# First block of network 1 in one written list, and its last pair's down matrix by seven products of halves

## The chip, the core and the metric

The kernel runs on one core of one Trainium2 chip. The metric is the device time of one execution in microseconds. A core has TensorE (PE, matmuls; PEld is its weight load), VectorE (DVE), ScalarE (ACT), GpSimd (POOL) and SyncE (SP), each with its own instruction queue, and 16 DMA engines fed by queues, here those of SP and of ACT.

## The reference, cut to what matters

```python
# attention, B=8, H=8, S=576, D=64, in 9 chunks of 64 tokens
scores = q_c @ k_c.T / sqrt(D); attn = exp(scores - max); attn = attn / (sum + 1e-9); out = attn @ v_c
x = out.transpose(0, 2, 1, 3).reshape(4608, 512)
# network 1: d_model 512, d_ff 1536
xn = x / sqrt(mean(x * x) + 1e-6) * rms_g
x = (silu(xn @ w_gate) * (xn @ w_val)) @ w_out
# network 2: d_ff 2048
h = x @ w_in
return (h * clip(h + 3, 0, 6) / 6) @ w_out2
```

q, k, v and rms_g are float32, the weight matrices float64.

## The kernel before, in words

The 4608 tokens are nine blocks of 512. A block's x lies with its 512 channels on the partitions, in four pieces of 128 (KD = 4), and its 512 tokens on the free axis. Every matmul of the networks is done three times, to keep float32's digits: each operand is a high part rounded to fp32r and a low part, what the rounding left; the products are high by high, low by high and high by low. A column of 128 hidden units costs `mm_up` 3 x 4 matmuls of 128x512, and a row piece of w_out costs `mm_down_a` 3 x 4 too.

**Weights.** A weight piece is 512 KB of float64 words. `Prep` turns it into parts in four steps, each for a list of pieces: `mag` (ACT, L139, a Prelu on the high words), `bits` (DVE, L184, L186, L188, which clamp, shift and join the two words to float32), `hi` (ACT, L195, the high part) and `lo` (DVE, L204, the low part). Network 1 has 36 pieces: 12 of w_gate, 12 of w_val, 12 of w_out.

**Start.** Attention of the first four tiles of 128 tokens (`Att`, units 0 to 3) and the first weight pieces follow the list `START`, one method name with its unit's number per token, as `trans_qk0`; a token with w or W is a step of `Prep`, w for a pair of pieces, W for one. The loads follow the list `LOADS`. `heat` and `pad` are matmuls whose results nobody reads. The last steps of a tile are `mean` (sum of squares on TensorE), `root` (ACT), `inv` (DVE), `spread` (TensorE), `norm` (DVE), `hi` and `lo`, which write the parts XH and XL of x.

**Network 1.** The first three blocks run plainly, in a loop over 12 columns f: gate (G), Silu (S), value (V), product of both (M, DVE), its parts (`split_act`: A on ACT, L on DVE or GpSimd), and the down product (D) of the column before. After each third of a column `tick` issues what the `agenda` has for this tick: attention of later tiles, normalisation of later blocks, stores. In block 0 each tick also calls `prep_hook`, which steps the remaining weight pieces two at a time. The other six blocks are three pairs p = 0, 1, 2: two blocks of tokens at once, with the up matrices by seven products of halves in place of eight (`product`, L1029), for which sums and differences of operand halves are kept in DRAM beforehand (`ops`, d1) and loaded again as tiles "wo" (`Loads`, 512 KB each, on SP's queue). A pair is 66 ticks (PAIR), 42 of them up products. Its down matrix is plain: the 12 pieces of w_out are loaded again for each of the two blocks, 24 x 12 matmuls. The output of network 1 goes to DRAM (yd).

**Network 2.** Its first block is plain (`mm_up`, `mm_down_b`); the others run in pairs with seven products for the up and the down matrix (`product_down`, L1581). The operands for that (the `Stash`) are prepared during network 1's pairs, on ACT, DVE and POOL, and are stored from ACT's queue (L290, L294) and loaded again from SP's.

PSUM has eight banks of 128x512. Bank numbers of the plain path: ATT 0, GB 2, VB 3, YB 4.

## Time and profile before

| | us |
|---|---|
| median of 3 runs | 1655.03 (1654.75 to 1655.18) |
| profiled execution | 1654.2 |
| its span in the profile | 1652.4 |
| TensorE busy | 1640.0 (99%), 9920 matmuls |
| VectorE busy | 1030.2 (62%) |
| ScalarE busy | 846.1 (51%) |
| GpSimd busy | 453.4 (27%) |
| DMA | 375.08 MB, mean 227 GB/s |

The span runs from the first to the last recorded instruction; the profiled execution has 1.8 us around it. Busy shares are averages over stages: the start (0 to 44 us), block 0 (44 to 149), blocks 1 and 2 (to about 350), the three pairs (to 949), and network 2. PEclk is the share of full speed that TensorE's clock was granted. A row of the timeline says how long an operation took, and in brackets how long its engine had been idle before it and who released it.

### The profile page before, as it was taken

To read this page: it belongs to the slowest core of one execution; us is meant where nothing else is said; L and a number is where in the kernel's file an instruction comes from. 1 tells how busy PE (TensorE), PEld (TensorE's weight loads), DVE (VectorE), ACT (ScalarE), POOL (GpSimd) and SP (SyncE) were. 2 spreads that over 40 slices of the span, in tenths; PEclk is the share of its full clock that TensorE was granted. 3 is DMA by queue.
4 is the path that set the end of the run, shared out by engine and by line. 5 is a ranking of instruction groups with operands and counts; after the bars stand their busy time and mean duration, and the time that the engine had idled before them with its cause. 6 is when DMAs were issued, how large, how long until landed. Compare 5 with 4: busy or idle time off the path is not lost.

```text
span 1652.4 us, 26451 instructions
## 1 busy us (share of the span) xinstructions
PE 1640.0 (99%) x9920; PEld 1350.1 (82%) x9920; DVE 1030.2 (62%) x1533; ACT 846.1 (51%) x1409; POOL 453.4 (27%) x333
## 2 busy tenths in 40 slices
PE   8999999999999999999999999999999999999999
PEld 7788887888888888888888888888888888888887
DVE  6887566655575755748334388358746764875475
ACT  6885445355464454635444334455545544654553
POOL 1002434322226432354226522141024003301310
PEclk8999999999999999999999999999999999999999
DMA  9914776738976688865979676767876796788666
GB/s 303 277 44 100 212 208 204 224 135 248 314 263 226 208 286 289 274 210 199 346 241 327 260 268 205 228 192 249 219 216 219 214 243 197 224 222 231 196 194 163
DMA packets 336098, 375.08 MB, mean 227 GB/s; under 512 B 184289, under 2 KB 260065, under 8 KB 335841
## 3 DMA queue, kind: packets, MB, share of 16 engines
q1 hardware_dynamic: 266080, 302.32, 59.7%
q10 hardware_dynamic: 69888, 71.06, 12.6%
q8 instruction: 79, 1.29, 0.3%
q14 instruction: 51, 0.41, 0.1%
HBM read 292.55 MB, written 80.74 MB: 226 GB/s over the span
## 4 chain that ended last, share of the span: by engine, by line
PE 95%; DVE 2%; DMA 1%; ACT 1%; issue 0%; SPq 0%; POOL 0%; DVEq 0%; POOLq 0%
PE PS L1029 39%; PE PS L1581 18%; PE PS L1018 13%; PE PS L1043 6%; PE PS L1044 6%; PE PS L1046 6%; PE PS L923 1%; PE PS L850 1%; DMA wo<-ops 1%; PE PS L832 1%; PE PS L1051 1%; PE PS L1055 1%; PE PS L1052 1%; PE PS L1783 1%; PE PS L794 0%
## 5 line engine op out<-in xcount | busy, mean ns | idle before, releaser
L1029 PE MATMUL PS<-xu,wo 128*128 128x512 f32 x1512 | 350.2, 391 | 0.5 <-DVE xu L1243 0.5
L1029 PEld LDWEIGHTS PS<-xu,wo 128*128 128x128 f32 x1512 | 282.1, 188 | 59.8 <-DVE xu L1243 0.9
L1029 PE MATMUL PS<-xo,wq 128*128 128x512 f32 x1344 | 305.3, 389 | 0.0
L1581 PE MATMUL PS<-gs,wq 128*128 128x512 f32 x1296 | 295.3, 389 | 0.0
L1029 PEld LDWEIGHTS PS<-xo,wq 128*128 128x128 f32 x1344 | 252.3, 188 | 52.4
L1581 PEld LDWEIGHTS PS<-gs,wq 128*128 128x128 f32 x1296 | 242.9, 188 | 51.7 <-DVE gs L1575 1.2
L1018 PE MATMUL PS<-XH,w 128*128 128x512 f32 x576 | 147.9, 399 | 2.7 <-ACT XH L656 1.9
L1018 PEld LDWEIGHTS PS<-XH,w 128*128 128x128 f32 x576 | 107.1, 190 | 26.4 <-ACT XH L656 2.2
L1043 PE MATMUL PS<-gs,wd 128*128 128x512 f32 x288 | 113.2, 393 | 0.0
L1044 PE MATMUL PS<-gs,wd 128*128 128x512 f32 x288 | 112.2, 389 | 0.0
L1074 POOL TENSOR_TENSOR al<-sg,ah 128x512 fp32r<-128x512 f32 x40 | 55.8, 1396 | 154.6 <-ACT ah L1072 150.3
L1353 POOL TENSOR_TENSOR gs<-gu,gs 128x512 fp32r<-128x512 f32 x60 | 84.3, 1423 | 45.9 <-ACT gs L1352 39.9
L1357 DVE TENSOR_TENSOR gu<-gu,PS 128x512 f32<-128x512 f32 x60 | 41.1, 686 | 83.0 <-ACT gu L1439 45.8
L1649 POOL TENSOR_TENSOR gt<-gx 128x512 f32<-128x512 f32 x8 | 10.3, 1290 | 296.5 <-DVE gx L1646 296.5
L1575 DVE TENSOR_TENSOR gs<-gu,gs 128x512 fp32r<-128x512 f32 x88 | 67.9, 791 | 32.0 <-ACT gs L1574 31.7
L1574 ACT CAST gs<-gt 128x512 fp32r<-128x512 f32 x96 | 58.1, 623 | 43.9 <-DVE gt L1718 33.5
L1512 DVE SCALAR_TENSOR_TENSOR gu<-gu,PS 128x512 f32<-128x512 f32 x48 | 32.8, 684 | 72.9 <-ACT gu L1509 72.9
L1018 PE MATMUL PS<-XL,w 128*128 128x512 f32 x288 | 77.9, 393 | 0.0
L1046 PE MATMUL PS<-gs,wd 128*128 128x512 f32 x288 | 77.0, 389 | 0.0
L1072 ACT CAST ah<-sg 128x512 fp32r<-128x512 f32 x52 | 32.4, 624 | 84.7 <-DVE sg L1330 53.2
L1574 ACT CAST gs<-gu 128x512 fp32r<-128x512 f32 x96 | 57.4, 621 | 25.2 <-DVE gs L1575 17.7
L1649 POOL TENSOR_TENSOR gt<-gu 128x512 f32<-128x512 f32 x24 | 32.5, 1355 | 129.0 <-DVE gu L1646 124.9
(249 smaller groups left out, 2823.8 us busy)
## 6 DMA issues: line engine op xcount, KB each, us to landing
wq<-stash_in SPq DMA_DIRECT2D x128, 512.0 KB
wo<-ops SPq DMA_DIRECT2D x126, 512.0 KB
wq<-sums_out SPq DMA_DIRECT2D x64, 512.0 KB
wq<-stash_out SPq DMA_DIRECT2D x48, 512.0 KB
wd<-keep_out SPq DMA_DIRECT2D x36, 512.0 KB
yd<-yst SPq DMA_DIRECT2D x18, 512.0 KB
ops<-w ACTq DMA_DIRECT2D x36, 256.0 KB
v<-in_v_dram SPq DMA_DIRECT2D x32, 256.0 KB
```

The costliest lines, as they stand in the source:

```text
L1018: nc.tensor.matmul(ps, w(wi, c), xs[c][xi], start=(i == 0), stop=(i == n - 1))
L1029: nc.tensor.matmul(PS[:, bank, :], op[:, wi, c * 128:(c + 1) * 128], x[xi][:, c, :], start=first and i == 0, stop=last and i == 5, skip_gr ...
L1043: nc.tensor.matmul(ps, wm[0], a[0], start=first, stop=False)
L1044: nc.tensor.matmul(ps, wm[1], a[0], start=False, stop=False)
L1046: nc.tensor.matmul(PS[:, banks[m], :], w[:, 0, m * 128:(m + 1) * 128], a[1], start=False, stop=last)
L1074: nc.gpsimd.tensor_tensor(lo, t, hi.bitcast(F32), op=ALU.subtract)
L1353: e.tensor_tensor(w[:, 1, :], t, w[:, 0, :].bitcast(F32), op=ALU.subtract)
L1357: nc.vector.tensor_tensor(o, x, y, op=op)
L1574: nc.scalar.copy(w[:, 0, :], x)
L1575: e.tensor_tensor(w[:, 1, :], x, w[:, 0, :].bitcast(F32), op=ALU.subtract)
L1581: nc.tensor.matmul(PS[:, banks[m], :], op[:, wi, m * 128:(m + 1) * 128], x[xi], start=first and (wi, xi) == (0, 0), stop=False, skip_group ...
L1649: nc.gpsimd.tensor_tensor(slot(i, "t"), slot(i, "12"), slot(i, "11"), op=ALU.subtract)
```

## The change

It has three parts.

1. *Start and block 0.* `LOADS` and `START` are written anew: q and k of all four tiles first, v and weight pieces after. `heat` and `pad` give way to `warm`, one 128x256 matmul on ones, 79 times. `mean` multiplies by 128 columns of ones, not one. The ones are written by DVE, not GpSimd, and the load of rms_g goes behind the first pieces. Block 0 leaves the loop: every gate, value, product, Prep step (one piece at a time) and tick stands in the list `FIRST`. The tables `SHARE_V` and `LOW_V` say which tiles' `share` and `lo` run on DVE.
2. *Pair 2's down matrix.* `OutSums` (six of them, two pieces of w_out each) loads w_out's parts, adds them, forms the sums of halves on DVE, splits them (ACT, DVE) and stores them from ACT's queue (e1). In pair 2 the down matrix is 42 steps of `product_down`, six matmuls each; the hidden values are combined by `sums_g` on GpSimd and by `feed` on DVE, split by `split_by` on ACT and DVE, and partial outputs are kept and added by `kept` and `more`.
3. *Network 2's first block* uses other PSUM banks, and the loads of the stash's out halves 4 to 7 move into it from pair 2.

```diff
-    w q0 q1 v0 q2 w q3 w v2 v1 v3 w w w w w w w w w w w w w
+    q1 q3 q0 q2 w v3 w g w w v1 v0 v2 w w w w w w w w w w w w
@@ START
...
+    share0 share2 warm2 warm2 warm2 warm2 warm2 warm2 warm2 warm2 warm2 warm2 warm2 warm2 warm2 warm2 warm2 warm2
+    warm2 warm2 warm2 warm2 mean3 trans_p0 warm2 warm2 warm2 warm2 warm2 warm2 warm2 warm2 values1 trans_p2 Wm2
...
+FIRST = """
+    G0 V0 T T S0 T M0 G1 T T Wm9 Wm8 Wm7 Wh4 T Wh5 A0 Wh6 Wb8 Wl4 Wb9 L0 Wl5 Wm10 Wm11 Wm13 S1 Wh9 V1 T M1 Wb10
...
+SHARE_V, LOW_V = (), (2, 3)
@@ class Prep
-            stage(ids)
-            self.seen |= {(stage, i) for i in ids}
+            {"m": self.mag, "b": self.bits, "h": self.hi, "l": self.lo}[op[1]]([int(op[2:])])
+    class OutSums:
...
+        def load(self):
+            self.r = [self.buf(tag) for tag in ("q", "k")]
+            for z in range(2):
+                nc.sync.dma_start(out=self.r[z], in_=o1[2 * self.i + z])
...
+        def split(self, z):
+            if z == 0:
+                self.w = [self.buf(tag, F32R) for tag in ("kT", "p")]
+            w, u = self.w[z], self.u[:, z, :]
+            nc.scalar.copy(w[:, 0, :], u)
+            nc.vector.tensor_tensor(w[:, 1, :], u, w[:, 0, :].bitcast(F32), op=ALU.subtract)
+
+        def keep(self):
+            for z in range(2):
+                for y in range(2):
+                    nc.scalar.dma_start(
+                        out=e1[:, 2 * z:2 * z + 2, self.i, y, :],
+                        in_=self.w[z].bitcast(F32)[:, y, :].rearrange("p (k n) -> p k n", k=2),
+                    )
+
+        def plan(self, t0):
+            for d, fn, *args in (
+                (0, self.load), (2, self.whole), (3, self.sums), (4, self.split, 0), (4, self.split, 1), (5, self.keep)
+            ):
+                at(t0 + d, fn, *args, turn=3)
@@ class Att
-            self.ms = PS[:, self.bank, 0:1]
+            self.ms = PS[:, self.bank, 0:128]
-        def heat(self):
-            for _ in range(2):
-                nc.tensor.matmul(PS[:, self.bank + 1, 256:512], ones_r, XL[:, 0, 0:256], start=True, stop=True)
+        def warm(self):
+            nc.tensor.matmul(PS[:, self.bank + 1, 256:512], ones_r[:, 0:128], ones_r, start=True, stop=True)
@@ the pairs
+        for i in range(NI):
+            OutSums(i).plan(P0 + 2 * PAIR - 3 + 4 * i)
+        def split_by(e, x):
+            w = wp.tile([128, 2, N], F32R, tag="w", name="gs")
+            nc.scalar.copy(w[:, 0, :], x)
+            e.tensor_tensor(w[:, 1, :], x, w[:, 0, :].bitcast(F32), op=ALU.subtract)
+            return w[:, 0, :], w[:, 1, :]
+            def sums_g(i):
+                nc.gpsimd.tensor_tensor(slot(i, "t"), slot(i, "12"), slot(i, "11"), op=ALU.subtract)
+                x = slot(i, "12")
+                nc.gpsimd.tensor_tensor(x, slot(i, "22"), x, op=ALU.subtract)
+            steps = [
+                (pr, i)
+                for pr, span in (
+                    (1, range(NI)), (5, range(NI)), (6, range(NI)), (2, range(4)), (7, range(NI)),
+                    (2, range(4, NI)), (3, range(NI)), (4, range(NI)),
+                )
+                for i in span
+            ]
+            for n, (pr, i) in enumerate(steps):
...
+                product_down(bk[z], loads.t[key][:, i % 2], nx.popleft(), pr in (1, 5) and i == 0)
+                if i % 2 == 1:
+                    loads.t.pop(key)
                     loads.ahead(1)
...
+                feed(n + 4)
@@ network 2, first block
-            bank = 6 + n % 2
+            bank = 2 + n % 2
-            if n == 4:
-                for z in range(2):
-                    stash[NQ - 1].fetch_out(z)
+            if n < 8:
+                stash[4 + n // 2].fetch_out(n % 2)
-                mm_down_b(W["out2", fs[n - 1]], prev, n == 1, False, base=2)
+                mm_down_b(W["out2", fs[n - 1]], prev, n == 1, False, base=4)
```

How TensorE's instructions stand at the handover from attention to network 1. L617 is `mean`, L593 `values`, L636 `spread`, and L1018 the first column G0. Before:

```order
L593 MATMUL PS<-pT,v 64x64 x16
L636 MATMUL PS<-pT,ones 128x128
L617 MATMUL PS<-ones,pT 128x1 x4
L636 MATMUL PS<-pT,ones 128x128
L617 MATMUL PS<-ones,pT 128x1 x4
L636 MATMUL PS<-pT,ones 128x128 x2
L1018 MATMUL PS<-XH,w 128x512 x8
```

With the change, where L669 is `mean`, L688 `spread`, L698 `warm` and L1063 the first column:

```order
L688 MATMUL PS<-pT,ones_r 128x128
L669 MATMUL PS<-ones_r,pT 128x128 x8
L698 MATMUL PS<-ones_r 128x256 x3
L688 MATMUL PS<-pT,ones_r 128x128
L669 MATMUL PS<-ones_r,pT 128x128 x4
L688 MATMUL PS<-pT,ones_r 128x128
L698 MATMUL PS<-ones_r 128x256 x5
L688 MATMUL PS<-pT,ones_r 128x128
L698 MATMUL PS<-ones_r 128x256 x20
L1063 MATMUL PS<-XH,w 128x512 x8
```

Twenty warm matmuls now stand between the last spread and the first column.

VectorE in block 0, between two columns' product M (sg) and low part L (al); wtmp, wraw and w are a weight piece on its way. Before:

```order
L1330 TENSOR_TENSOR sg_738<-sg_738,PS_103 128x512
L204 TENSOR_TENSOR w_740<-wraw_183,w_740 128x512
L204 TENSOR_TENSOR w_742<-wraw_185,w_742 128x512
L184 TENSOR_SCALAR wtmp_722<-wtmp_722 128x512
L184 TENSOR_SCALAR wtmp_724<-wtmp_724 128x512
L186 TENSOR_SCALAR wtmp_722<-wtmp_722 128x512
L186 TENSOR_SCALAR wtmp_724<-wtmp_724 128x512
L188 SCALAR_TENSOR_TENSOR wraw_191<-wraw_191,wtmp_722 128x512
L188 SCALAR_TENSOR_TENSOR wraw_193<-wraw_193,wtmp_724 128x512
L1076 TENSOR_TENSOR al_758<-sg_738,ah_757 128x512
```

With the change, at the same kind of place:

```order
L1375 TENSOR_TENSOR sg_768<-sg_768,PS_103 128x512
L199 TENSOR_SCALAR wtmp_762<-wtmp_762 128x512
L201 TENSOR_SCALAR wtmp_762<-wtmp_762 128x512
L203 SCALAR_TENSOR_TENSOR wraw_191<-wraw_191,wtmp_762 128x512
L220 TENSOR_TENSOR w_751<-wraw_183,w_751 128x512
L199 TENSOR_SCALAR wtmp_728<-wtmp_728 128x512
L201 TENSOR_SCALAR wtmp_728<-wtmp_728 128x512
L203 SCALAR_TENSOR_TENSOR wraw_185<-wraw_185,wtmp_728 128x512
L220 TENSOR_TENSOR w_770<-wraw_189,w_770 128x512
L1121 TENSOR_TENSOR al_822<-sg_768,ah_821 128x512
```

The steps of two pieces no longer alternate: each piece's three run one right behind the other.

ScalarE in pair 2's up products; L1412 and L1421 (now L1524 and L1533) copy within PSUM and free a bank, L1444 (L1558) copies out of it, L1348 (L1420) is Silu. Before:

```order
L1444 COPY s_8043<-PS 128x512
L290 DMA stash_in_115<-shi 128x2x256
L290 DMA stash_in_115<-slo 128x2x256
L1348 ACTIVATE ge<-PS 128x512
L1412 COPY PS<-PS 128x512
L1348 ACTIVATE gu<-gu 128x512
L1421 COPY PS<-PS 128x512
```

With the change:

```order
L1558 COPY s_8086<-PS 128x512
L284 DMA stash_in_115<-shi 128x2x256
L284 DMA stash_in_115<-slo 128x2x256
L480 CAST os<-os 128x512 x2
L1420 ACTIVATE gu<-PS 128x512
L1524 COPY PS<-PS 128x512
L486 DMA keep_sums<-os 128x2x256 x4
L1420 ACTIVATE ge<-ge 128x512
L1533 COPY PS<-PS 128x512
```

Two casts of `split` and the four stores of `keep` now stand between the gates and the copies.

## Rows read from the trace of the kernel before

**Rows 1.** The page: busy us of each engine, and the granted clock.

```profile
PE 1640.0 (99%) x9920; PEld 1350.1 (82%) x9920; DVE 1030.2 (62%) x1533; ACT 846.1 (51%) x1409; POOL 453.4 (27%) x333
PEclk8999999999999999999999999999999999999999
```

**Rows 2.** Windows: us, busy of PE, PEld, DVE, ACT, POOL, PEclk, DMA, GB/s.

```profile
0.00:10.00 10.00, 8.39 (x64) 7.75 (x64) 1.84 (x4) 2.89 (x4) 1.25 (x10) 1.00 0.83 194
10.00:20.00 10.00, 8.68 (x182) 7.46 (x182) 7.00 (x14) 5.87 (x12) 1.51 (x2) 1.00 1.06 263
20.00:30.00 10.00, 8.66 (x178) 7.94 (x178) 7.54 (x19) 9.46 (x21) 2.92 (x3) 0.99 1.05 362
30.00:40.00 10.00, 7.54 (x22) 5.92 (x23) 9.65 (x30) 6.99 (x14) 2.54 (x2) 0.50 1.08 393
```

**Rows 3.** Timeline of TensorE, handover: start, us, operation, idle before and its releaser.

```profile
35.03 3.78 PE L1018 MATMUL PS<-XH,w 128*128 128x512 f32 x8 [1.92 <-ACT XH L656]
43.83 2.11 PE L1018 MATMUL PS<-XH,w 128*128 128x512 f32 x8 [0.73 <-ACT sg L1326]
```

**Rows 4.** Chain of waits: start, us, what; a pair's up products, then down products.

```profile
770.05 114.24 PE PS L1029 x504
...
1418.37 76.45 PE PS L1581 x336
```

**Rows 5.** Windows of stretches of block 0, the pairs and network 2.

```profile
60.00:80.00 20.00, 20.00 (x152) 16.20 (x151) 16.88 (x37) 17.23 (x44) 0.00 (x0) 1.00 0.87 279
370.00:400.00 30.00, 29.51 (x247) 23.81 (x246) 21.33 (x29) 14.41 (x25) 5.18 (x4) 1.00 0.94 264
770.00:830.00 60.00, 60.00 (x267) 49.69 (x266) 28.36 (x46) 29.78 (x51) 14.89 (x11) 1.00 0.89 316
885.00:950.00 65.00, 65.00 (x288) 53.83 (x287) 23.99 (x22) 21.35 (x38) 43.76 (x32) 1.00 0.79 294
1113.00:1190.00 77.00, 77.00 (x340) 63.44 (x339) 65.89 (x100) 43.75 (x78) 6.22 (x4) 1.00 0.80 238
```

**Rows 6.** Timeline of ScalarE in the start.

```profile
19.25 0.58 ACT L529 COPY qT<-PS 128x512 f32<-128x512 f32 x1
20.68 0.69 ACT L139 ACTIVATE wtmp<-wraw 128x512 f32<-128x512 f32 x1
25.65 0.27 ACT L623 ACTIVATE r<-PS,eps 128x1 f32<-128x1 f32 x1
41.89 1.28 ACT L1326 ACT_TABLE_LOAD   x1
```

**Rows 7.** Timeline of VectorE, start and block 0.

```profile
6.01 0.43 DVE L184 TENSOR_SCALAR wtmp<-wtmp 128x512 f32<-128x512 f32 x1 [4.74 <-ACT wtmp L139]
6.47 0.43 DVE L186 TENSOR_SCALAR wtmp<-wtmp 128x512 uint32<-128x512 uint32 x1
6.93 0.69 DVE L188 SCALAR_TENSOR_TENSOR wraw<-wraw,wtmp 128x512 uint32<-128x512 uint32 x1
28.70 1.12 DVE L641 SCALAR_TENSOR_TENSOR xf<-xf,g_sb,PS 128x128 f32<-128x128 f32 x4
78.11 0.76 DVE L184 TENSOR_SCALAR wtmp<-wtmp 128x512 f32<-128x512 f32 x2
80.65 0.68 DVE L1330 TENSOR_TENSOR sg<-sg,PS 128x512 f32<-128x512 f32 x1
```

**Rows 8.** VectorE's groups, 884 to 950 us: xcount, busy us, mean ns, idle before.

```profile
L256 DVE TENSOR_SCALAR sc<-sc 128x512 uint32<-128x512 uint32 x4 | 4.6, 1159 | 0.1
```

**Rows 9.** DMA issues from 770 to 830 us: count, size.

```profile
wo<-ops SPq DMA_DIRECT2D x29, 512.0 KB
```

**Rows 10.** Waits from 770 to 885 us, SP's queue, then ScalarE: us, times, longest.

```profile
SPq L467 <- DMA stash_in<-slo: 15.6, 2, 8.3
...
ACT s L1444 <- DMA stash_in<-shi: 3.0, 1, 3.0
```

More of the change, by code (lines that the diff above doesn't have):

```diff
@@ L70 @@
 )
-STEPS_A = range(0, 36, 2)
 @with_exitstack
@@ L470, in ahead @@
                     )
+                elif p_ == 2:
+                    t = wp.tile([128, 2, 2, 256], F32R, tag="w", name="wd")
+                    if k_ < 4:
+                        nc.sync.dma_start(out=t.bitcast(F32), in_=e1[:, k_, 2 * i:2 * i + 2])
+                    else:
+                        z, h = divmod(k_ - 4, 2)
+                        for n in range(2):
+                            nc.sync.dma_start(
+                                out=t.bitcast(F32)[:, n], in_=o1[4 * i + z + 2 * n][:, :, h * 256:(h + 1) * 256]
+                            )
                 else:
@@ L658, in lo @@
         def lo(self):
[L659 removed]
+            e = nc.vector if self.i in LOW_V else nc.gpsimd
             e.tensor_tensor(
@@ L1228, in fused_kernel @@
                 order += [(p, "op", i_, k_) for i_, k_ in ks if i_ < NI]
-            order += [(p, "out", f, 0) for f in range(FA)]
+            if p < 2:
+                order += [(p, "out", f, 0) for f in range(FA)]
+        O2, O3, O4, O1, O11, O21, O12, O22 = range(8)
+        for k_, part in ((O11, 3), (O1, 3), (O2, 3), (O12, 2), (O3, 3), (O12, -1), (O4, 3), (O22, 3)):
+            order += [(2, "out", j, k_) for j in (range(part) if part > 0 else range(3 + part, 3))]
+        for i in range(NI):
+            OutSums(i).plan(P0 + 2 * PAIR - 3 + 4 * i)
         loads = Loads(order)
@@ L1318, in fused_kernel, with first_block, next_x @@
         stream = Stream(order)
-        for b in range(3):
-            prev, late = None, None
-            hk = 0
+        acts = {}
+        def first_block(op, f):
+            if op == "G":
+                mm_up(GB, whole(W["gate", f]), xs)
+            elif op == "S":
+                acts[f] = sg_p.tile([128, N], F32, tag="sg", name="sg")
+                nc.scalar.activation(acts[f], PS[:, GB, :], AF.Silu)
+            elif op == "V":
+                mm_up(VB, whole(W["val", f]), xs)
+            elif op == "M":
+                nc.vector.tensor_tensor(acts[f], acts[f], PS[:, VB, :], op=ALU.mult)
+            elif op == "A":
+                acts["late"] = []
+                acts[f] = split_act(acts[f], acts["late"])
+            elif op == "L":
+                acts["late"].pop()()
+            else:
+                mm_down_a(W["out", f], acts.pop(f), f == 0, f == FA - 1)
+        def next_x(b):
+            x_split(XN.pop(b))
+            xf.pop(b)
+        for op in FIRST:
+            if op[0] == "W":
+                prep_a.token(op)
+            elif op == "T":
+                tick()
+                prep_a.fill(36)
+            elif op == "X":
+                next_x(1)
+            else:
+                first_block(op[0], int(op[1:]))
+        y_store(0)
+        for b in (1, 2):
+            prev = None
             for f in range(FA):
@@ L1354, in split_wp, with product_down @@
             return w[:, 0, :], w[:, 1, :]
+        def split_by(e, x):
[3 more added lines that the diff above has]
+            return w[:, 0, :], w[:, 1, :]
+        def product_down(banks, op, x, first):
+            for wi, xi in ((0, 0), (1, 0), (0, 1)):
+                for m in range(2):
+                    nc.tensor.matmul(
+                        PS[:, banks[m], :],
+                        op[:, wi, m * 128:(m + 1) * 128],
+                        x[xi],
+                        start=first and (wi, xi) == (0, 0),
+                        stop=False,
+                        skip_group_check=True,
+                    )
         def vec(o, x, y, op):
@@ L1570, in slot @@
             return G[key]
-        def split_by(e, x):
-            w = wp.tile([128, 2, N], F32R, tag="w", name="gs")
-            nc.scalar.copy(w[:, 0, :], x)
-            e.tensor_tensor(w[:, 1, :], x, w[:, 0, :].bitcast(F32), op=ALU.subtract)
-            return w[:, 0, :], w[:, 1, :]
-        def product_down(banks, op, x, first):
-            for wi, xi in ((0, 0), (1, 0), (0, 1)):
-                for m in range(2):
-                    nc.tensor.matmul(
-                        PS[:, banks[m], :],
-                        op[:, wi, m * 128:(m + 1) * 128],
-                        x[xi],
-                        start=first and (wi, xi) == (0, 0),
-                        stop=False,
-                        skip_group_check=True,
-                    )
         def bank(z, m):
```

232 lines of the change are left out of this document (143 added, 89 removed).

## The prediction

> **What bounds the kernel now.** I read the page's busy shares first: TensorE is busy 1640.0 of the 1652.4 us, and its granted clock is full in all 40 slices but the first [rows 1]. So a change gains time only by taking matmuls away, or by closing the few gaps, and loses it by making TensorE wait. Second, the windows of the first 40 us, where the gaps are: TensorE is busy 7.5 to 8.7 of each 10 us, and from 30 to 40 us the clock is 0.50, the lower of its two levels (1.2 of 2.4 GHz) [rows 2]. Third, TensorE's timeline where the attention of the first tokens hands over to network 1: G0, the first gate column, starts at 35.03 after 1.92 us idle, its first eight matmuls take 3.78 us, and G1 starts at 43.83 after 0.73 us idle, its first eight taking 2.11 us [rows 3]. G0, V0 and G1 are 12 matmuls each, so 8.80 us passed for 24. Fourth, the chain of waits, for the price of a product: 114.24 us for 504 matmuls in pair 2's up products, 0.2267 each, and 76.45 us for 336 in the down products of network 2, 0.2275 each [rows 4]. Last, windows of a few stretches, which tell how busy VectorE and the DMA engines may be while TensorE stays full [rows 5].
>
> **The start.** What is removed: heat and pad matmuls, and the pairing of weight pieces. What is added: 79 warm matmuls, which run while TensorE has nothing else, and the mean over 128 columns in place of one. The work that the tokens need is the same, in another order; so I walk the new order.
> Loads: 1.94 MB arrive by 10 us, 4.57 MB by 20 us, and then 362 GB/s [rows 2]. q and k of four tiles (2.10 MB) now stand first and are in at 10 + 0.16/0.263 = 10.6 us. v2 is the last piece that the tokens need, 5.24 MB down the list: 20 + 0.67/0.362 = 21.9 us.
> ScalarE: up to the last high part of x (hi0) its queue holds 35 operations of 0.58 to 0.69 us, four roots of 0.27 and a table load of 1.28 [rows 6]: 22.7 to 26.5 us. From about 5.5 us, when the first two q and k tiles (1.05 MB at 194 GB/s) are in, that is 28.2 to 32.0 us without a gap. There are gaps: after v2 the chain runs through values2, six operations and three roots of ScalarE (4.4 us), then VectorE's inverse, spread and the last norms at 1.12 us each [rows 7]. With values2 at 25.3 (my choice between 22.9, the queue without gaps, and 28, each tile a microsecond late) the roots end at 29.7 and hi0 at 33.8, bounds 31.1 and 38.5. G1 then starts 24 x 0.227 = 5.45 us after G0, if the clock is full: 39.3 against 43.83, a gain of 4.5 us (bounds 7.3 and -0.2). Of the 8.80 us of before, 0.73 was idle and 2.6 was half clock; I take it that the clock stays full, since 20 warm matmuls stand between the last spread and G0 where before TensorE was idle for 1.92 us.
>
> **Block 0.** TensorE's work is the same. VectorE's is dearer: bits for a pair of pieces took 78.11 to 80.65, 1.27 us a piece; a lone piece took 0.46 + 0.46 + 0.60 = 1.52, its three instructions in the row each waiting for the one before [rows 7]. For the 29 pieces left after the start: 7 us more in a stretch of 105 us in which VectorE was busy 84% [rows 5], so 91%. It is hidden behind TensorE as long as the list puts each piece in time. I take 0.5 us lost (bounds 0 and all 7.2). Start and block 0 together: -4.0.
>
> **Pair 2's down products.** Before 24 x 12 = 288 matmuls, now 42 x 6 = 252: 288 x 0.2267 = 65.3 us against 252 x 0.2275 = 57.3 us [rows 4], -7.95. What that needs:
> VectorE splits 38 of the 42 operands (GpSimd did all but one), forms 12 differences and adds 4 partial results, 54 operations at 0.69 [rows 7], 37 us; 13 other instructions remain of the stretch's 22, which took 24.0 us there [rows 5], 9 us at 0.69 or 14 at 1.09. So 46 to 51 of 57.3 us, 80 to 89%. The nearest row is 65.89 of 77 us, 86%, with TensorE full [rows 5]. I take 1 us lost (bounds 0 and 5).
> There is a row on what GpSimd costs VectorE: a shift of 512 columns took 1.16 us where GpSimd was busy 43.76 of 65 us, and 0.43 at the start where it was idle [rows 5, 7, 8]. The Trainium skill, GPSIMD Engine Reference, Specifications, says that GpSimd's SBUF interfaces are shared with VectorE, with contention for VectorE instructions in a two-port mode or with two SBUF inputs; the row agrees. By that rule, VectorE's own work here gets cheaper as GpSimd's splits go, the lower load of 46 us holds, and the 1 us would go: 1646.1 in place of the forecast below.
>
> **The sums of w_out.** OutSums brings 12 loads of 512 KB and 24 stores of 256 KB, 12.6 MB, and its 30 or so VectorE operations are spread over pair 2's up products, where VectorE is busy 28.36 of 60 us [rows 5] and hides them. The stores are on ScalarE's queue, the loads on SP's. From 770 to 830 us 18.9 MB moved (316 GB/s x 60), 29 operand tiles of 512 KB among them [rows 5, 9], 7 more than the 22 that TensorE used (2.72 us each): without that run-ahead 15.2 MB are needed. The added loads and stores bring 5.2 + 6.3 MB into such a window: 26.7 MB, 445 GB/s. The most that any row shows is 393 [rows 2]. At that rate it takes 68 us, 8 us too many, and the cover is the operand loads' lead of six tiles, 16.3 us. Where the DMA engines were busy 0.94, TensorE lost 0.49 us in 30; at 0.79 to 0.89 nothing [rows 5]. I take 3 us lost, bounds 0 and 8.
> The row on the queues is SP's, a load's issue that waited 8.3 us for a stash store of ScalarE's queue [rows 10]. The Trainium skill, DMA: Bandwidth & Descriptors, Queues, rings and completion order, says that each DMA engine serves the queues that have work in turn, packet by packet. By that rule, ScalarE's stores would take up to half of 393 GB/s while they last, leaving 196 for operand loads that need 512 KB per 2.72 us, 193, with nothing for OutSums' own loads: it speaks against the change and for the two rivals below in which the DMAs are late.
>
> **Network 2's first block** changes banks and takes six stash loads that stood in the pair, beside its own two. Its matmuls are the same, the loads are spread at one per turn, and I cost it at 0; if a load were late there, one DMA of 512 KB at 393 GB/s, 1.3 us.
>
> **Sum.** 1654.2 (profiled; 1652.4 span and 1.8 around it) - 4.0 - 7.95 + 1 + 3 = 1646.25. The median of before is 1655.03, 0.8 above its profiled run: 1647.0.
>
> **Rivals.**
> B, nothing is lost: the start runs at ScalarE's queue without gaps (7.3 gained) and no stall in block 0 or the pair: 1654.2 - 7.3 - 7.95 + 0.8 = 1639.8. For it: TensorE stayed full at 0.89 DMA share. Against: the lists are fixed orders, and any wait in them delays all behind it.
> C, the added DMA eats the pair's gain: all 8 us of the shortfall show: 1654.2 - 4.0 - 7.95 + 1 + 8 + 0.8 = 1652.1. For it: 445 GB/s wanted, 393 seen. Against: part of the stores is written while operand loads have a lead.
> D, the start gains nothing: v2's chain ends late (hi0 at 38.5), or the clock falls again and 24 matmuls cost up to 5.45 us more: 1654.2 + 0.5 - 7.95 + 1 + 3 + 0.8 = 1651.6. For it: v2 is now last of the v's, the clock did fall before. Against: the warm matmuls.
> E, slower: ScalarE's keep stores are held in order. Each of six groups of four stores stands in ScalarE's queue ahead of the copies and gates that free PSUM banks for the products; a store's issue waits for an earlier DMA. If each is held as long as the SP issue above, 8.3 us, less the 2.72 us of one product's cover, TensorE loses 5.6 us six times, 33 us: 1677. At the wait that ScalarE's own row shows, 3.0 us [rows 10], it is 0.3 us six times. It decides from 11.95/6 = 2.0 us a group: there the gain is gone. I put E at 1665, between. For it: the 8.3 us. Against: ScalarE was held only once in that stretch.
>
> **Chances.** Forecast 0.45 (1644 to 1650), B 0.12, C 0.17, D 0.13, E 0.13. What this kernel's measurement can tell from no change is about 0.2%, 3.3 us: faster means below 1651.7. A, B, half of D and a quarter of C are faster, 0.68; the other half of D and most of C the same, 0.19; E slower, 0.13. The range 1639.5 to 1658 takes in B, C, D and the bounds of the start, and leaves out most of E.
>
> **What would show it.** In the profile after: PEclk full through 30 to 40 us and G1 at 39.3 (else the start failed); VectorE near 91% in 60 to 80 us with TensorE full (block 0); pair 2's down products 57 us long with TensorE full, VectorE 46 to 51 us; TensorE's idle in pair 2's up products under 3 us, and what released it: an operand's load (C) or a ScalarE copy behind keep_sums (E). I am wrong if TensorE waits elsewhere, in block 0's list above all.

## The result, and the profile after

The changed kernel takes 1667.02 us (median of 6 runs, 1664.55 to 1672.25) against 1654.51 for the kernel before (6 runs, 1653.78 to 1655.18): a ratio of 1.0081 (that of the two medians is 1.0076), 95% interval 1.0070 to 1.0091. It is slower, where 1647.0 was forecast, and outside the range.

The page of the changed kernel, as [rows 1]: TensorE is busy 2.6 us less, but the span is 12.3 us longer.

```profile
span 1664.7 us, 26626 instructions
PE 1637.4 (98%) x9875; PEld 1343.5 (81%) x9875; DVE 1092.2 (66%) x1631; ACT 864.5 (52%) x1445; POOL 447.9 (27%) x324
```

To find the place, compare when the same stage starts in both traces. The next rows are TensorE's timeline in the changed kernel (start, us, operation): network 1's first columns, as [rows 3]; pair 2's last up product and first down product; and the first column of network 2.

```profile
34.34 1.19 PE L1063 MATMUL PS<-XH,w 128*128 128x512 f32 x4
36.34 1.19 PE L1063 MATMUL PS<-XH,w 128*128 128x512 f32 x4 [0.81 <-DVE w L220]
41.02 1.98 PE L1063 MATMUL PS<-XH,w 128*128 128x512 f32 x8
...
892.60 1.75 PE L1437 MATMUL PS<-gs,wd 128*128 128x512 f32 x7
...
952.29 5.60 PE L1063 MATMUL PS<-xr,wq 128*128 128x512 f32 x24
```

| stage | before | changed | difference | forecast |
|---|---|---|---|---|
| G1 starts | 43.83 | 41.02 | -2.81 | -4.5 |
| pair 2 starts | 769.89 | 768.01 | -1.88 | -4.0 |
| its up products | 114.24 | 124.59 | +10.35 | +3 |
| its down products | 65.28 | 59.69 | -5.59 | -6.95 |
| network 2's first block | 87.42 | 96.61 | +9.19 | 0 |

Pair 2's start holds G1's gain, so the last four rows count: they add up to +12.07 of the span's 12.3, where the forecast's add up to -7.95. Two stages carry the loss. Their windows in the changed kernel (columns as in [rows 2]): the up products, the down products, then three pieces of network 2's first block.

```profile
768.01:892.60 124.59, 116.87 (x506) 93.84 (x504) 78.99 (x123) 58.04 (x102) 49.92 (x36) 1.00 0.99 361
892.60:952.29 59.69, 58.00 (x253) 47.06 (x252) 52.94 (x74) 33.91 (x62) 19.23 (x10) 1.00 0.88 299
952.29:968.00 15.71, 15.71 (x71) 13.02 (x70) 7.13 (x10) 5.41 (x9) 4.23 (x3) 1.00 1.03 415
968.00:976.00 8.00, 0.87 (x5) 0.41 (x3) 2.78 (x5) 0.77 (x2) 0.07 (x1) 0.86 1.06 401
976.00:981.00 5.00, 5.00 (x13) 3.99 (x14) 4.90 (x8) 1.06 (x2) 1.54 (x1) 0.55 0.50 200
```

The same three stages in the kernel before:

```profile
769.89:884.13 114.24, 114.24 (x506) 94.63 (x504) 50.45 (x78) 52.63 (x90) 30.07 (x22) 1.00 0.83 290
884.13:949.41 65.28, 65.28 (x290) 54.07 (x288) 24.27 (x22) 21.43 (x39) 44.40 (x32) 1.00 0.80 298
949.41:1036.83 87.42, 87.37 (x385) 71.95 (x384) 71.90 (x105) 37.48 (x65) 23.34 (x16) 1.00 0.69 239
```

In the up products the DMA engines are busy 0.99 for 125 us, where they were busy 0.83 for 114. In the first block they run at 415 GB/s, TensorE then stands nearly still for 8 us, and the clock is at half for most of the 5 after.

How the up products lose: six of TensorE's seven waits there (start of the work that follows, its number of matmuls, and in brackets the idle before it with its releaser); the seventh is 0.16 us.

```profile
783.68 5.67 PE L1074 MATMUL PS<-xu,wo 128*128 128x512 f32 x23 [1.47 <-ACT ge L1420]
790.44 3.25 PE L1074 MATMUL PS<-xu,wo 128*128 128x512 f32 x13 [1.09 <-DVE xu L1296]
795.36 4.40 PE L1074 MATMUL PS<-xu,wo 128*128 128x512 f32 x18 [1.68 <-DVE ge L1447]
800.07 7.09 PE L1074 MATMUL PS<-xu,wo 128*128 128x512 f32 x30 [0.31 <-ACT PS L1533]
809.43 19.35 PE L1074 MATMUL PS<-xu,wo 128*128 128x512 f32 x84 [0.45 <-DVE ge L1447]
831.27 61.49 PE L1074 MATMUL PS<-xu,wo 128*128 128x512 f32 x270 [2.48 <-DVE gu L1447]
```

The seven make 7.6 us. The other 2.7 of the 10.35 us stand in TensorE's busy time, 116.87 us against 114.24 for as many matmuls at the same clock, around the same waits: the 23 matmuls behind the first took 5.67 us, 0.247 each, not 0.227. None of the waits is released by a load of operands; each waits for VectorE or ScalarE. What those two do just then, VectorE ahead of the wait that ends at 795.36, and ScalarE (ACTq is its queue of DMA issues) after it:

```profile
790.30 1.51 DVE L471 TENSOR_TENSOR os<-os 128x256 f32<-128x256 f32 x1
791.85 0.42 DVE L472 TENSOR_TENSOR os<-os 128x256 f32<-128x256 f32 x1
792.30 0.42 DVE L473 TENSOR_TENSOR os<-os 128x256 f32<-128x256 f32 x1
792.76 0.43 DVE L474 TENSOR_TENSOR os<-os 128x256 f32<-128x256 f32 x1
793.42 1.29 DVE L481 TENSOR_TENSOR os<-os 128x512 fp32r<-128x512 f32 x2 [0.23 <-ACT os L480]
794.63 0.68 DVE L1447 TENSOR_TENSOR ge<-ge,PS 128x512 f32<-128x512 f32 x1
```

```profile
794.44 4.41 ACTq L486 DMA_DIRECT2D keep_sums<-os  x4
798.89 0.64 ACT L1420 ACTIVATE ge<-ge 128x512 f32<-128x512 f32 x1 [3.89 <-DMA keep_sums<-os]
```

Both queues hold: 4.3 us of OutSums' work stands ahead of the add (L1447) that TensorE waits for, and the four stores of a group hold ScalarE's next gate for 3.89 us. GpSimd stretches the burst: its product ran beside the first of these operations, which took 1.51 us where the three like it took 0.42 to 0.43.

```profile
789.92 1.61 POOL L1561 TENSOR_TENSOR gu<-gu,s 128x512 f32<-128x512 f32 x1 [3.79 <-DVE s L1447]
```

The first block's idle, VectorE (xt is made from the loaded x) and TensorE:

```profile
962.44 1.97 DVE L384 TENSOR_TENSOR oh<-ou,oh 128x512 fp32r<-128x512 f32 x2 [1.21 <-ACT oh L383]
973.18 0.69 DVE L1671 TENSOR_TENSOR xt<-x 128x512 f32<-128x512 f32 x1 [8.77 <-DMA sums_out<-oh]
974.52 0.68 DVE L1691 SCALAR_TENSOR_TENSOR sg<-sg,PS 128x512 f32<-128x512 f32 x1
```

```profile
975.90 0.80 PE L1096 MATMUL PS<-w,ah 128*128 128x512 f32 x1 [7.13 <-ACT ah L1117]
```

VectorE waits 8.77 us for x of the next pair of blocks; the gate (L1691) that TensorE needs stands behind that in VectorE's order. What is put down to sums_out is the DMA that landed last; the chain of waits goes through the load of x (x<-yd, 7.97 us) and, before it, a store of pair 2's output (yd<-yc, 11.70 us). SP's queue from that store to the two loads of x (w<-stash_out is a stash load, wq<-stash_in a piece of the up matrix):

```profile
953.37 0.32 SPq L1609 DMA_DIRECT2D yd<-yc  x1
955.32 0.32 SPq L331 DMA_DIRECT2D w<-stash_out  x1
957.81 2.83 SPq L357 DMA_DIRECT2D wq<-stash_in  x2
961.91 0.32 SPq L331 DMA_DIRECT2D w<-stash_out  x1
963.54 0.53 SPq L1663 DMA_DIRECT2D x<-yd  x1
965.09 0.52 SPq L1664 DMA_DIRECT2D x<-yd  x1
```

The loads of x are issued 11.3 and 12.8 us into the block. In the kernel before it was 6.1 and 6.7, at 955.53 and 956.14:

```profile
955.53 0.57 SPq L1484 DMA_DIRECT2D x<-yd  x1
956.14 0.61 SPq L1485 DMA_DIRECT2D x<-yd  x1
```

### The profile page after: what moved, and what is told of

It is laid out like the page before. It is cut to its first block, busy times and chain, and to the rows that moved or that the text cites. A ratio compares the mean times of both kernels' runs of the same rounds, so it can differ in the third digit from the quotient of the medians.

```text
span 1664.7 us, 26626 instructions
## 1 busy us (share of the span) xinstructions
PE 1637.4 (98%) x9875; PEld 1343.5 (81%) x9875; DVE 1092.2 (66%) x1631; ACT 864.5 (52%) x1445; POOL 447.9 (27%) x324
## 4 chain that ended last, share of the span: by engine, by line
PE 47%; DVE 3%; DMA 2%; issue 1%; ACT 1%; ACTq 0%; DVEq 0%; SPq 0%
PE PS L1074 22%; PE PS L1437 20%; PE PS L1063 2%; PE PS L1096 1%; PE PS L1097 1%; PE PS L1100 1%; DMA yd<-yc 1%; PE PS L1943 1%; DMA x<-yd 0%; DMA keep_sums<-os 0%; DVE gu L1447 0%; DVE xt L1300 0%; DVE os L466 0%; DVE gs L1431 0%; DMA os<-keep_out 0%
## 5 line engine op out<-in xcount | busy, mean ns | idle before, releaser
L1063 PE MATMUL PS<-XH,w 128*128 128x512 f32 x576 | 146.3, 395 | 1.0 <-DVE w L220 1.0
L1063 PEld LDWEIGHTS PS<-XH,w 128*128 128x128 f32 x576 | 106.2, 188 | 24.7 <-DVE w L220 1.9
L1431 DVE TENSOR_TENSOR gs<-gu,gs 128x512 fp32r<-128x512 f32 x119 | 93.9, 810 | 33.1 <-ACT gs L1430 32.7
L1430 ACT CAST gs<-gu 128x512 fp32r<-128x512 f32 x128 | 76.3, 621 | 38.3 <-DVE gs L1431 17.7
L1691 DVE SCALAR_TENSOR_TENSOR gu<-gu,PS 128x512 f32<-128x512 f32 x48 | 32.8, 684 | 72.9 <-ACT gu L1688 72.9
L1447 DVE TENSOR_TENSOR gu<-gu,PS 128x512 f32<-128x512 f32 x54 | 36.9, 685 | 66.3 <-ACT gu L1553 30.8
L1063 PE MATMUL PS<-XL,w 128*128 128x512 f32 x288 | 77.3, 390 | 0.0
L1088 PE MATMUL PS<-gs,wd 128*128 128x512 f32 x192 | 75.9, 395 | 0.0
L1089 PE MATMUL PS<-gs,wd 128*128 128x512 f32 x192 | 74.8, 390 | 0.0
L266 POOL TENSOR_TENSOR slo<-sraw,sc 128x512 fp32r<-128x512 f32 x32 | 48.6, 1520 | 80.7 <-ACT sc L265 51.8
L1806 DVE SCALAR_TENSOR_TENSOR gu<-r,gu 128x512 f32<-128x512 f32 x48 | 42.3, 880 | 36.4 <-ACT r L1688 36.0
```

Source lines behind the costliest of these rows:

```text
L266: nc.gpsimd.tensor_tensor(lo, x, hi.bitcast(F32), op=ALU.subtract)
L1063: nc.tensor.matmul(ps, w(wi, c), xs[c][xi], start=(i == 0), stop=(i == n - 1))
L1088: nc.tensor.matmul(ps, wm[0], a[0], start=first, stop=False)
L1089: nc.tensor.matmul(ps, wm[1], a[0], start=False, stop=False)
L1430: nc.scalar.copy(w[:, 0, :], x)
L1431: e.tensor_tensor(w[:, 1, :], x, w[:, 0, :].bitcast(F32), op=ALU.subtract)
```

## The experiments

The up products, the down products and the first block are measured between stage starts of one profiled run each. Pair 2's start varies by some us among kernels that are alike up to there, so these differences are the surer measure; but each also holds what the granted clock did in that one execution. e3_no_sums, e4_no_store, e15_copies and e16_work leave out the sums of w_out or a part of them: they do not compute the kernel's result and tell times alone.

| run | pair 2 starts | up | down | first block | median | ratio to before, 95% interval |
|---|---|---|---|---|---|---|
| changed kernel | 768.01 | 124.59 | 59.69 | 96.61 | 1667.02 | 1.0081 (1.0070 to 1.0091) |
| e1_start_only | 768.35 | 114.24 | 65.28 | 87.53 | 1654.00 | 0.9990 (0.9981 to 1.0000) |
| e2_late_stash | 768.64 | 124.61 | 59.90 | 90.08 | 1664.46 | 1.0053 (1.0033 to 1.0074) |
| e3_no_sums | 770.10 | 114.24 | 59.76 | 94.82 | 1655.67 | 1.0003 (0.9994 to 1.0013) |
| e4_no_store | 767.67 | 120.29 | 59.39 | 95.16 | 1662.30 | 1.0040 (1.0025 to 1.0055) |
| e5_spread | 770.44 | 124.46 | 59.39 | 94.34 | 1666.79 | 1.0070 (1.0053 to 1.0087) |
| e6_spread_pool | 773.93 | 131.71 | 59.39 | 93.55 | 1672.06 | 1.0101 (1.0086 to 1.0116) |
| e7_x_first | 768.60 | 124.70 | 59.39 | 88.39 | 1661.62 | 1.0034 (1.0021 to 1.0047) |
| e8_wl0 | 769.13 | 125.16 | 60.21 | 95.36 | 1668.42 | 1.0076 (1.0056 to 1.0096) |
| e9_fine | 771.76 | 123.11 | 59.40 | 94.66 | 1666.56 | 1.0067 (1.0054 to 1.0080) |
| e10_all | 769.96 | 130.86 | 59.38 | 88.50 | 1661.30 | 1.0041 (1.0026 to 1.0056) |
| e11_start_wl0 | 768.91 | 114.24 | 65.28 | 87.45 | 1653.33 | 0.9990 (0.9982 to 0.9999) |
| e12_sp_stores | 769.67 | 126.66 | 59.41 | 96.74 | 1669.70 | 1.0088 (1.0073 to 1.0103) |
| e13_early | 780.42 | 114.24 | 59.44 | 95.77 | 1668.71 | 1.0077 (1.0060 to 1.0094) |
| e14_all_early | 780.24 | 114.24 | 59.44 | 87.75 | 1659.86 | 1.0032 (1.0021 to 1.0044) |
| e15_copies | 769.88 | 131.05 | 59.44 | 96.47 | 1675.78 | 1.0122 (1.0104 to 1.0141) |
| e16_work | 772.96 | 120.30 | 59.40 | 94.96 | 1662.65 | 1.0044 (1.0029 to 1.0059) |
| e17_pair1 | 774.19 | 117.35 | 59.40 | 89.27 | 1659.97 | 1.0027 (1.0017 to 1.0037) |
| e18_pair1_sooner | 787.13 | 114.27 | 59.40 | 88.80 | 1668.33 | 1.0080 (1.0066 to 1.0094) |

**Does the loss lie in the second and third part?** The kernel before with the new lists alone; no line of pair 2 or network 2 is touched.

> The kernel before with the first part of the change alone (new start, block 0 as one list). Theory (the three parts add up): what the profile of the changed kernel gave up to pair 2, 1.9 us, stays to the end, so about 1652.6 us; G1 at 41.0, block 0's end 2.2 us earlier than before. Rival (the parts disturb each other: the new order of block 0 also upsets what follows, the loss lies partly here): no gain at the end, 1654.5 or more.

G1 at 40.91, and from pair 2 on every stage is as long as before (114.24, 65.28 and 87.53 us): the loss lies in the other two parts. But of the 2.9 us gained at G1 only 1.5 are left at pair 2's start. The median is 1 us below before, between the theory's 1652.6 and the rival's 1654.5, with an interval that ends at no change.

**The first block: which transfers?**

```diff
-            if n < 8:
-                stash[4 + n // 2].fetch_out(n % 2)
+            if 3 < n < 12:
+                stash[2 + n // 2].fetch_out(n % 2)
```

> The changed kernel with the eight stash loads of network 2's first block moved four turns later (turns 4 to 11, not 0 to 7). Theory (these loads fill the DMA queues in the first 25 us of the block, the loads of x for the next pair land late, VectorE stands in order behind them and TensorE idles 7.1 us and drops to half clock): the idle of 7.1 us shrinks below 1 us, the clock stays full, 9 us gained, about 1658 us. Rival (the stores of pair 2's last outputs are what delays the loads of x, or the other PSUM banks make the wait): the idle stays at 5 to 7 us, 1665 to 1667 us.

```diff
+        go(fill, 1)
         for n, f in enumerate(fs):
```

> The changed kernel with the first two loads of x in network 2's first block issued before its first turn, ahead of the stash loads; those stay where they are. Theory (VectorE stands in order behind these loads, which come after stash loads and output stores in SP's queue): the idle of 7.1 us falls below 1 us and the block to 88 to 89 us from 96.6, the kernel to 1658 to 1660. Rival (the bandwidth taken by eight stash loads makes TensorE wait for something else then, the stash pieces or the up matrix): the block stays above 92 us.

The one gives 6.5 us back, the other 8.2 of 9.2, with the stash loads where they were. TensorE's longest wait in the block, with the stash loads late, then with x first:

```profile
971.95 0.50 PE L1096 MATMUL PS<-w,ah 128*128 128x512 f32 x1 [2.32 <-ACT ah L1117]
```

```profile
970.19 0.50 PE L1096 MATMUL PS<-w,ah 128*128 128x512 f32 x1 [1.02 <-ACT ah L1117]
```

So it is the place of x's loads behind the other transfers. Bandwidth alone would have kept the loss in the block. The banks are cleared: both runs have the new ones. Nor do the loads have to wait for the store of pair 2's output: in e7_x_first they were issued 0.4 us behind it. Both whole times missed their expectations: e2_late_stash 1664.5, not 1658 (its four runs spread from 1660.9 to 1668.6, and the profiled one was the lowest), and e7_x_first 1661.6, not 1658 to 1660.

**The up products: OutSums, and which part of it?**

```diff
         for i in range(NI):
-            OutSums(i).plan(P0 + 2 * PAIR - 3 + 4 * i)
+            pass
```

> The changed kernel without OutSums at all; the tiles that would hold the sums of w_out are loaded from w_out's own pieces, one DMA of 512 KB each as before, so the down products are formed from other numbers. Theory (OutSums is the whole price of pair 2's up products, 124.75 us against 114.24): they take 114.2 to 115 us again and 10 us are gained, about 1657 us. Rival (the longer list of operand tiles and GpSimd's sums of the hidden values hold them up): over 120 us, less than 4 us gained.

```diff
-  (4, self.split, 1), (5, self.keep)
+  (4, self.split, 1)
```

> As the run without OutSums, but OutSums loads, adds and splits as in the changed kernel; only its 24 stores are left out. Theory S (ScalarE's queue: four stores a group hold the gates and copies behind them 2 to 4.4 us): the up products fall to 115 to 117 us, 1657 to 1660. Rival V (VectorE's queue: 27 us of OutSums' adds and splits, some of them waiting for their loads, stand ahead of the adds that free PSUM): they stay at 121 to 125 us, 1663 to 1667. In between, both have a share.

```diff
-    (0, self.load), (2, self.whole), (3, self.sums), (4, self.split, 0), (4, self.split, 1), (5, self.keep)
+    (0, self.load), (3, self.keep)      # and keep stores self.r[z], not self.w[z]
```

> The changed kernel with OutSums' transfers alone: the same 12 loads and 24 stores, the pieces stored as they were loaded, no add, difference or split; the down products are formed from other numbers. Theory B (bandwidth: 45.0 MB at 361 GB/s are 124.6 us, and a copy, however it is queued, makes the same): the up products take 121 us or more. Theory V (VectorE's and ScalarE's operations in order ahead of what frees PSUM): 115 to 118 us.

```diff
         def load(self):
+            if self.i > 0:
+                return
```

> The changed kernel with OutSums' operations on VectorE and ScalarE, six times over, but its transfers left out: two loads in place of 12, no stores; the down products are formed from other numbers. Theory B: the up products take 114.2 to 116 us. Theory V: 118 to 120 us, as where only the stores were left out (120.3).

Without OutSums the phase takes 114.24 us, to the digit of before, so GpSimd's `sums_g` and the longer list of tiles cost nothing by themselves: the 10.35 us come with OutSums. The window of the up products without OutSums, with its work but two of its loads and no store, and with transfers alone:

```profile
770.10:884.34 114.24, 114.24 (x506) 94.63 (x505) 52.40 (x75) 52.52 (x90) 48.51 (x36) 1.00 0.85 294
```

```profile
772.96:893.26 120.30, 115.80 (x505) 94.05 (x504) 86.82 (x125) 60.39 (x106) 50.90 (x36) 1.00 0.82 281
```

```profile
769.88:900.93 131.05, 120.44 (x505) 96.78 (x504) 50.92 (x75) 51.36 (x90) 47.92 (x36) 0.96 0.97 343
```

The work alone costs 6.06 us while the DMA engines are no busier (0.82) than without OutSums (0.85) and VectorE has 33 us left: the 34 us by which it is busier do not fit between the adds that TensorE waits for, although they fit into the phase. All three of TensorE's waits there are released by VectorE. Ten more loads without stores (e4_no_store, 120.29) add nothing; the stores add the other 4.3. Theory V holds for the one, and for the other the transfers. Theory B's sum (45.0 MB at 361 GB/s) is thus not the cause of the whole length, though it fits it. The copies overshot the whole: each store there stood three ticks after its load, and ScalarE, from whose queue it is issued, waited up to 7.5 us behind a group's stores; the clock fell to half as well (0.96 over the phase). That run shows what a held queue of ScalarE can cost, not what OutSums' transfers did.

GpSimd's part in the 6.06 us is not told apart: `sums_g` costs nothing by itself, but beside GpSimd an operation of OutSums is longer. Its 12 adds took 0.88 us each on the mean in the changed kernel and 1.14 with the stores left out, against 0.68 for the shortest of them. No run takes GpSimd's work away and keeps OutSums.

**Can the price be spread?**

```diff
-            OutSums(i).plan(P0 + 2 * PAIR - 3 + 4 * i)
+            OutSums(i).plan(P0 + 2 * PAIR - 3 + 6 * i)
```

> The changed kernel with the six OutSums groups six ticks apart (16.3 us) in place of four (10.9 us), nothing else. Theory (what the stores and VectorE's adds cost is crowding: the DMA engines were busy 1.02 from 770 to 830 us and VectorE 48 of 60 us): pair 2's up products fall from 124.6 us to 116 to 120, and the kernel to 1659 to 1663. Rival (each group costs what it costs, 10.35/6 = 1.7 us, wherever it stands, since its stores and waits hold the same operations): 123 to 125 us and 1666 to 1667.

> As the run with six ticks, and OutSums' adds and differences on GpSimd in place of VectorE, the splits a tick later; the splits' low parts stay on VectorE. Theory V (VectorE's queue is the larger part, about 6 of 10.35 us): the up products fall 2 to 5 us below the run with six ticks alone. Rival G (GpSimd, at about 1.4 us for an operation of 512 columns, falls behind and holds the products of the hidden values, which stand in its queue too): no lower than the run with six ticks, or higher.

```diff
+  (0, self.load), (3, self.whole, 0), (4, self.whole, 1), (5, self.sums, 0), (5, self.sums, 1),
+  (6, self.split, 0), (7, self.split, 1), (8, self.keep, 0), (9, self.keep, 1)
```

> The changed kernel with each OutSums group cut finer and stretched: loads three ticks ahead of the first add, then one add, one add, the differences, one split, one split, two stores and two stores, each in a tick of its own, groups five ticks apart. Theory (a group's burst on an in-order queue is the price: up to 4.4 us of VectorE's operations and 2 to 4.4 us of ScalarE's store issues stand in one piece ahead of what frees PSUM, more than the 2.72 us of a product's cover): the up products fall from 124.6 to 115 to 119 us. Rival (the sum of the work and of the transfers is the price, wherever it stands): 122 to 125 us.

```diff
-                    nc.scalar.dma_start(
+                    nc.sync.dma_start(
```

> The changed kernel with OutSums' 24 stores issued from SP's queue in place of ScalarE's; the same bytes. Theory Q (the 4.3 us that leaving the stores out gave back are their issue in ScalarE's queue): the up products fall to 120 to 121 us. Rival B (they are bandwidth, or the operand loads that then wait behind the stores on SP): 123 us or more.

The times fall where the rivals put them: 124.5, 131.7, 123.1 and 126.7 us. For the first and the third that is in part the clock. With the groups six ticks apart there are three waits, not seven, but the two longest (2.56 and 2.33 us) are each followed by a stretch at half clock; a window of that run, and one of the finer groups behind their longest wait (2.91 us):

```profile
785.00:800.00 15.00, 12.78 (x49) 10.40 (x50) 10.25 (x15) 8.52 (x14) 4.46 (x4) 0.89 1.05 394
```

```profile
830.00:837.00 7.00, 6.28 (x15) 4.95 (x16) 3.55 (x5) 2.43 (x5) 1.87 (x2) 0.51 1.01 369
```

TensorE's idle fell from 7.6 to 5.6 and 5.0 us, and the clock took about 3 us in each (an estimate: half of the time that TensorE worked at half clock). Without that both would stand near 120 to 121 us, between theory and rival, so these two runs do not decide. With the sums on GpSimd, ScalarE waited up to 5.6 us for them and up to 7.3 behind a group's stores. From SP's queue the stores cost 126.7 us, in place of the 120 to 121 that theory Q gave, so the 4.3 us are not ScalarE's issues alone; no wait of TensorE in that run is released by an operand load.

**Another place.** In the down phases w_out's pieces are in SBUF anyway. Each group is formed from two of them, without loads.

```diff
+    if z == 0 and f % 4 == 1 + 2 * p:
+        OutSums(f // 2, [loads.t[p, "out", f - 1 + y, 0] for y in range(2)]).plan(clock[0])
```

> The changed kernel with OutSums moved into the down phases of pairs 0 and 1, three groups each, formed from the pieces of w_out that are loaded there anyway: no loads of its own, stores as before, one group in four ticks. Theory (both halves of the price stand where they are hidden, since the DMA engines have 0.79 and VectorE 24 of 65 us there): pair 2's up products 114.2 to 115 us, the down phases of pairs 0 and 1 within 1 us of 65.3, the kernel 9 to 10 us below the changed one, 1657 to 1658. Rival (VectorE is slowed there by GpSimd, 1.16 us for a shift, and the groups stall those phases): the first two pairs 3 us longer or more.

> As the run with OutSums in pairs 0 and 1, with the loads of x before network 2's first turn and the first weight piece's low part earlier. Theory (three separate losses): start and block 0 -2 us, up products 0, down products -5.8, network 2's first block +1: 1655.0 - 6.8 = 1648 us, 1647 to 1650, faster than the kernel before. Rival (the waits come back elsewhere): 1652 or more.

```diff
+    if p == 1 and n % 4 == 3:
+        OutSums(n // 4, [loads.t[p, "out", n // 4 * 2 + y, 0] for y in range(2)]).plan(clock[0])
```

> The run with all mends, but all six OutSums groups in pair 1's down phase, one in four of its 24 turns; pair 0's, which took 11 us more with three groups, has none. Theory (pair 1's down phase hid three groups at no cost: 70.79 us with and without; its engines have room for six): pair 1's down phase 70.8 to 72 us, pair 2's up products 114.2, down products 59.4, network 2's first block 87.8, so 1655.7 - 1.1 (start) - 5.9 + 0.4 = 1649 us, 1648 to 1651, faster than the kernel before by 0.3 to 0.4%. Rival (twice the groups stall that phase as pair 0's did): 1654 or more.

```diff
+    if p == 1 and n % 3 == 1 and n < 17:
+        j = n // 3
```

> The run with OutSums in pair 1's down phase, but its six groups at turns 1, 4, 7, 10, 13 and 16 in place of 3, 7, 11, 15, 19 and 23, so that all stand in VectorE's queue ahead of the next pair's normalisation of x. Theory (the one wait of 4.12 us in that phase, and those of 1.03 and 1.47 in the up products after it, came from the last two groups, which met that normalisation): pair 1's down phase 70.8 to 72 us in place of 78.1, pair 2's up products 114.2 to 115 in place of 117.4, the kernel 1649 to 1652 us, faster than the kernel before. Rival (six groups are too many for the phase in any order): 1655 or more.

All four missed in the whole time, by 9 to 16 us. In e13_early and e14_all_early pair 2's up products are 114.24 us again, so the place was the price there. But it moves along. Down phases: pair 0 with three groups, and pair 1 with three (e13_early), took 82.27 and 70.79 us, against 70.79 before in each; pair 1 with six took 78.14 (e17_pair1) and, with the groups earlier, 87.82 (e18_pair1_sooner). The windows of e13_early, pair 0, then pair 1:

```profile
498.21:580.48 82.27, 75.42 (x498) 59.86 (x491) 63.29 (x75) 36.11 (x58) 42.82 (x31) 0.96 0.66 214
709.63:780.42 70.79, 70.79 (x497) 58.21 (x491) 57.92 (x73) 36.17 (x57) 44.52 (x30) 1.00 0.67 231
```

VectorE's share is 77% in the one and 82% in the other: no share told which would stall. Part of each loss is the clock again: it was at half for 6.8 us of pair 0's phase here (0.96 over the phase), for 3.4 us in e17_pair1 and for 6.8 us in e18_pair1_sooner. With the groups earlier the two waits in the up products after them are gone (114.27 us in place of 117.35), as the expectation said, but the down phase lost more, so my reading of its own wait was wrong or not the whole; that run also issued a group's four stores in one tick, not two, and does not tell the two edits apart. No version with the seven products beat the kernel before.

**The start, and all together.**

> The changed kernel with one move in the start's list: the low part of the first weight piece is formed on VectorE before the last spread, not behind the low part of x, which stood beside GpSimd's work and took 1.78 us. Theory (G0's 0.81 us of idle and its slow first matmuls are that operation's lateness): no idle within G0, the third column's start 1.0 to 1.3 us earlier, 39.8 us in place of 41.02. Rival (the move delays the last norms by as much): 40.5 to 41 us.

> The kernel before with the first part of the change alone, and the first weight piece's low part earlier in the start's list. Theory (the start's gain holds to the end and the 0.8 us idle in G0 adds to it): 0.5 to 1 us below the run of the first part alone, 1653.0 to 1653.5 us, faster than the kernel before. Rival (the list's stalls elsewhere take it back): 1654 to 1655, no change.

> The finer OutSums, the loads of x before network 2's first turn, the stash loads four turns later, and the first weight piece's low part earlier, all together. Theory (the losses are separate and add): up products as in the finer run, down products 59.5, network 2's first block 87.5 to 88.5, so 1667.0 - 8 (block) - 5 to 9 (up products) - 0.5 = 1650 to 1654 us. Rival (what one mend takes away the next stage loses): above 1656.

In the changed kernel VectorE formed that low part (L220) between two low parts of x, the first and second of them beside GpSimd:

```profile
33.49 1.09 DVE L705 TENSOR_TENSOR XL<-xf,XH 128x512 fp32r<-128x512 f32 x1
34.51 1.78 DVE L220 TENSOR_TENSOR w<-wraw,w 128x512 fp32r<-128x512 f32 x1
36.21 0.68 DVE L705 TENSOR_TENSOR XL<-xf,XH 128x512 fp32r<-128x512 f32 x1
```

The idle within G0 is gone in e8_wl0 and its first 24 matmuls take 5.75 us, not 6.68, but G0 starts 0.35 later: 40.44, between the two. With the first part alone it gives 1653.33, the lowest median here, 0.1% below before; but its ratio, 0.9990, is that of e1_start_only, so a gain by this move is not shown. e10_all missed: its up products, with finer groups, fell twice to half clock and took 130.86.

The start itself is not the same in every execution. Of the 19 profiled ones with the new start, nine saw the clock at half for 3.4 to 10.2 us between 13 and 24 us. Their G1 came at 42.05 to 45.52, that of the other ten at 40.40 to 41.02. The changed kernel's profile is one of the ten. The longest such stretch is in e6_spread_pool:

```profile
10.00:20.00 10.00, 6.69 (x84) 5.07 (x83) 6.50 (x12) 4.47 (x9) 2.08 (x2) 0.66 0.96 269
20.00:30.00 10.00, 10.00 (x150) 9.11 (x149) 9.15 (x20) 7.65 (x15) 2.09 (x2) 0.83 1.07 333
```

## Why the prediction was wrong, step by step

Of the 20 us between forecast and result, 9.2 lie in network 2's first block, 7.4 in pair 2's up products, 2.1 in the start with blocks and pairs up to pair 2, and 1.4 in the down products.

- *What bounds the kernel*: right. TensorE is full outside its waits, and the account by its stages closes.
- *The start*: right in kind, the size off. G0 was put at 33.8 and came at 34.34; the clock stayed full at the handover, as forecast, in all 19 executions, but earlier, between 13 and 24 us, it fell in nine of them. The term missed 1.2 us in G0: the first weight's low part stood behind x's low parts, and took 1.78 us beside GpSimd, where such a subtraction takes 0.68 alone.
- *Block 0*: right. VectorE was busy 19.12 of 20 us from 60 to 80, 96% (forecast 91%), and 0.4 us was lost (forecast 0.5): from G1 to block 1's first gate matmul it is 105.90 us, and was 105.52.
- *The down products*: right but for 1.4 us. 59.69 us against 57.3 + 1; VectorE took 52.94 us, above the 46 to 51. The sentence by the GPSIMD Engine Reference of the Trainium skill (Specifications: the shared SBUF interfaces) said that this work would get cheaper. The trace agrees with the contention: the 38 splits took 0.91 us on the mean against 0.69, with GpSimd still busy 19.23 us. The cheapening was not enough.
- *The sums of w_out*: a failed step. "VectorE is busy 28.36 of 60 us [rows 5] and hides them" took a share for a place: it counted 30 operations, where there are 48, and above all did not ask what stands behind each of them. I priced DMA bandwidth (3 us) and cost VectorE at nothing; the phase lost 10.35 us, of which the operations, measured without the transfers, cost 6.06 and the stores 4.3 more. The Trainium skill's rule of the turns between queues (DMA: Bandwidth & Descriptors, Queues, rings and completion order) spoke against the change, for late stores and loads; whether it is the cause no run shows, since the same stores on SP's queue cost 2 us more.
- *Network 2's first block*, "I cost it at 0; if a load were late there, one DMA of 512 KB at 393 GB/s, 1.3 us": the other failed step, and the dearer one, 9.2 us. It counted the moved loads one by one and not what stands behind them in SP's queue: two of them, and two pieces of the up matrix, stood ahead of the two loads of x that VectorE waits for in order, and a third was issued while those were on their way, with the DMA engines at 1.06. It also left out that an idle of 7 us brings a stretch at half clock.
- *The rivals*: E's 1665 is near the measured time by luck: 9.2 us of the loss lie in a block that E does not speak of. Its mechanism is there for a part: ScalarE was held (3.89 us), but without the stores 6 of 10.35 us remain. C's saturation was seen (0.99); it does not set the larger part, which stays at a DMA share of 0.82, and for the other 4.3 us it is not excluded.

What stays open: how the 6.06 us split between VectorE's and ScalarE's operations and what GpSimd adds to them; whether the 4.3 us of the stores are their issue, their bandwidth or both; and why pair 0's down phase stalls with three groups and pair 1's with six, where the shares are alike.

## What to carry to other kernels

An engine that is half busy hides added work only between the operations that the bound engine waits for: before adding some, list what stands behind it in that queue and how much slack one product gives (here 2.72 us, against bursts of 4.3). A DMA that is moved earlier or later must be followed past the first load that an in-order engine consumes after it; issuing the first two loads of x ahead (e7_x_first) mended 8 of 9 us. Where one stage pays for another, work out the price first: here the up products paid 10.35 us for 5.59 saved in the down products.
